# Delta rule attention and a gated feed-forward on one core: value scalings, fillers, key turns and weight conversion put in other places

## The chip, the cores and the metric

The kernel runs on one core of one Trainium2 chip. The time is device microseconds of one execution. Before the change it is 775.02 us, the median of three runs (773.91 to 776.28).

## The reference, cut to what matters

```python
k_n = k / (norm(k) + 1e-6)                      # batch 4, heads 8, sequence 768, head size 48
for t in range(768):
    y[t] = q[t] @ state
    v_old = k_n[t] @ state
    state += beta[t] * outer(k_n[t], v[t] - v_old)
x = y, heads side by side                       # 3072 x 384
h = x @ w_in                                    # 384 x 2048
out = (h * sigmoid(1.702 * h)) @ w_out          # 2048 x 384
```

The weights `w_in` and `w_out` reach the kernel as 64-bit floats and are turned into 32-bit ones on the chip by integer arithmetic; everything else is 32-bit.

## The kernel before, in words

**Units.** The sequence is cut into 6 chunks of 128 positions. A unit is one chunk of one batch with all its 8 heads: 24 units, number n = 4 c + b. For a unit the recurrence becomes a triangular solve: with the Gram matrix of its keys, `G`, and the inverses of the 32 x 32 blocks on its diagonal, `XB`, the values are solved block by block (4 blocks). A chunk's diagonal blocks are inverted for all its batches at once by `invert` (line 440), a long series of multiply and reduce pairs on VectorE (DVE). For the first chunk, which has no state, the norms of the keys are not applied to the keys but folded in as factors `zs` (lines 336 to 352); its values are multiplied by the norms with `act.mul`, one ScalarE (ACT) instruction for each head of each of the four units (lines 976 to 978).

**Hops.** `hops(a, b)` (line 985) takes two units through their four blocks in turn, 8 hops for a pair. A hop is a call of `together` (line 826): on TensorE (PE) `solve` for a block of one unit (result `psU`) and `below` for a block of the other (the product of `G` with what is solved, `psR`); then ACT copies `psU` to `US` (or `U` for the fourth unit), and DVE subtracts `psR` from `V`. The next hop needs both. The first chunk has two pairs: units 0 and 1 (loop at line 1022), then 2 and 3 (loop at line 1050). After a pair, `put_out` (line 993) makes the outputs (`psY`), the new state `ST`, and the rows `xT` for the feed-forward.

**Work written by hand between the hops.** Instructions are issued in the order of the program on every engine (`pinned`, line 100, whose line 102 carries nearly all instructions of the profile), so the order of the calls is the order of each queue:

- `fill(n)` (line 292) issues n steps of the weight conversion (`conversion`, line 203, chained by `conversions`, line 253). A piece of the weights takes five steps: p (mask of the exponent on DVE, then a Relu on ACT), t and f (fraction, DVE), or (sign, DVE, needs the Relu), fin (product, DVE). There are 9 pieces of `w_in` and 14 of `w_out`; the p of a piece is issued ahead of the last two steps of the piece before it. When a piece is done, `fetches` (line 279) may start the DMA of a later one.
- `preparing` is `keys()` (line 998): normalising the keys of units 4 to 8 (`normalize_mixed`, line 315: Square on ACT, `ssq` on DVE, a power on GpSimd (POOL), reciprocal and product on DVE), their turn by PE (`turn`, line 396: `psT`, copied to `kT`), and their Gram matrices (`gram`, line 373: `psG`, two ACT copies to `G`), with the DMAs by way of DRAM that bring the diagonal blocks to `NT`. It goes on by ticks, `ahead_of(preparing, 1)`; the tuple in line 1012 says at which tick each of the five units begins, and a unit takes a step at every second tick.
- `warm(n)` (line 132) issues n matmuls of 256 columns whose result nobody reads (`ps_warm`): fillers for PE. `NW`, `NA`, `NY`, `NU` (line 58) are their numbers.
- `feed()` (line 1037) issues half of a step of the feed-forward's first product: `hidden` (line 730) makes `ph` from `w_in` and `xT`, 3 products, and after each second half ACT applies the gate to `gT`. A product of this kernel is two matmul instructions in the profile.

**After the pairs.** The inverse of the second chunk, `invert(1)`, has 21 steps; the loop at line 1087 issues them and 25 feeds. Then come `fill(5)`, what is left of the feeds, and `woven` (line 870) for each unit to the end: a unit's hops with the two units beside it, the keys of the unit five ahead, and between them feed-forward work from `queue`, as much as `share` says. The first entry of `queue` is `both_written` (line 771), the second product of the feed-forward for units 0 and 1: `po` from `w_out` and `gT`, 16 steps of two products, each of which first issues conversion up to three steps ahead of it. The `ph`, `po` and `ps_warm` tiles share two banks.

**Buffers that the change touches.** `zs` lies in the single buffer `ksq`, which the Square of `normalize_mixed` also uses (line 951). `late_U` (line 949) takes the first 400 columns of a spare `gT` buffer of 1024 columns.

Of the kernel before, what the change touches and what calls it, by code (L numbers as in the profile page):

```python
# [8 lines left out]
F32 = mybir.dt.float32  # L9
# [9 lines left out]
def kernel(  # L19
# [21 lines left out]
    B, H, S, D = q.shape  # L41
# [4 lines left out]
    NP = H // 2  # L46
# [5 lines left out]
    HB = 2  # L52
# [2 lines left out]
    GB = 8  # L55

    XR = DP - D
    NW, NA, NY, NU = 14, 3, 34, 11
    NQ = DFF // 4
    NPC = DFF // 8  # L60
    NS = C * C + C
# [6 lines left out]
    wk = ctx.enter_context(tc.tile_pool(name="wk", bufs=2))  # L68
# [63 lines left out]
    def warm(n):  # L132
        ps = ps_moe.tile([128, 256], F32, tag="moe", name="ps_warm")
        for _ in range(n):
            pe.matmul(ps, lhsT=ones[:, 0:128], rhs=ones, start=True, stop=True)
# [156 lines left out]
    def fill(n):  # L292
        for _ in range(n):
            next(converting, None)
# [20 lines left out]
    def normalize_mixed(n):  # L315
        K = KN[n % len(KN)][:, :, 0:D]
        ksq = wk.tile([128, H, D], F32, tag="ksq", name="ksq", bufs=1)
        act.activation(ksq, K, ACT.Square)
        yield
        ssq = wk.tile([128, H], F32, tag="ssq", name="ssq", bufs=4)  # L320
        vec.tensor_reduce(ssq, ksq, axis=AX.X, op=ALU.add)
        rn = wk.tile([128, H], F32, tag="rn", name="rn", bufs=4)
        pool.tensor_tensor(rn, ssq, half, op=ALU.pow)
        yield
        vec.tensor_scalar(rn, rn, 1e-6, None, op0=ALU.add)
        vec.reciprocal(rn, rn)
        vec.tensor_tensor(K, K, rn.broadcast_to([128, H, D]), op=ALU.mult)
        yield
# [71 lines left out]
    def prepare(n):  # L400

        c, b = units[n]
        turn(n)
        yield 0.6
        G = gram(n)
        if c == 1:
            Nd = dram.tile([H * C * BS], F32, tag="Nd", name="Nd", bufs=4)
            for blk in range(NB):
                u = slice(blk * BS, (blk + 1) * BS)
                sync(out=Nd.rearrange("(h p k) -> p h k", p=C, k=BS)[u], in_=G[u, :, u])  # L410
            yield 0.0
            yield 0.9
            sync(
                out=NT[b * NB * H : (b + 1) * NB * H].rearrange("d i k -> d (i k)"),
                in_=Nd.rearrange("(d r) -> d r", r=BS * BS),
            )
            yield 0.0
            return
        Nd = dram.tile([H * NS], F32, tag="Nd", name="Nd", bufs=4)
        dma = sync if c < 3 else nc.sync.dma_start  # L420
        dma(
            out=Nd.rearrange("(h r) -> h r", r=NS)[:, 0 : C * C].rearrange(
                "h (p k) -> p h k", k=C
            ),
            in_=G,
        )
        dma(
            out=NT[b * NB * H : (b + 1) * NB * H],
            in_=Nd.rearrange("(d r) -> d r", r=NS // NB)[:, 0 : BS * C].rearrange(
                "d (i k) -> d i k", k=C  # L430
            )[:, :, 0:BS],
        )
        yield 0.9


    def spare(name):
        t = wk.tile([128, FQ, NTH], F32, tag="gT", name=name, bufs=GB)
        return t.rearrange("p f t -> p (f t)")
# [315 lines left out]
    def written(c, b0, gT):  # L754

        for i in range(HB):
            b = b0 + i
            po = ps_moe.tile([128, DM], F32, tag="moe", name="po")
            for f in range(FC):
                pe.matmul(  # L760
                    po, lhsT=gT[f // FQ][:, f % FQ, i * C : (i + 1) * C], rhs=w_out[:, f, :],
                    start=(f == 0), stop=(f == FC - 1),
                )
                if f % 2 == 1 and f < FC - 1:
                    yield 1.3
            o = wk.tile([128, DM], F32, tag="o", name="o")
            act.copy(o, po)
            nc.sync.dma_start(out=out[b * S + c * C : b * S + (c + 1) * C, :], in_=o)
            yield 1.3

    def both_written(c, gT):

        po = [ps_moe.tile([128, DM], F32, tag="moe", name="po") for _ in range(HB)]
        for n, f in enumerate(order):
            ahead = order[min(n + 3, FC - 1)]
            while ("out", ahead - ahead % 2 if 4 <= ahead < 8 else ahead) not in done:
                fill(1)
            for i in range(HB):
                pe.matmul(
                    po[i], lhsT=gT[f // FQ][:, f % FQ, i * C : (i + 1) * C], rhs=w_out[:, f, :],  # L780
                    start=(n == 0), stop=(n == FC - 1),
                )
            if n < FC - 1:
                yield 1.3
        for i in range(HB):
            o = wk.tile([128, DM], F32, tag="o", name="o")
            act.copy(o, po[i])
            sync(out=out[i * S + c * C : i * S + (c + 1) * C, :], in_=o)
        yield 1.3
# [11 lines left out]
    def run(work):  # L801
        for _ in work:
            pass

    def ahead_of(work, n):
        for _ in range(n):
            next(work, None)
# [9 lines left out]
    def new_step(n):  # L817
        if n >= len(units):
            return NoStep()
        h = n // HB  # L820
        if h not in xTs:
            xTs[h] = wk.tile([128, KC, NTH], F32, tag="xT", name="xT", bufs=3)
        steps[n] = Step(n, xTs[h])
        return steps[n]

    def together(solves, belows):

        solves = [(X, blk) for X, blk in solves if X]
        belows = [(X, blk) for X, blk in belows if X]
        psU = bank("psU") if solves else None  # L830
        psR = bank("psR") if belows else None
        for h in range(H):
            for X, blk in solves:
                X.solve(blk, h, psU)
            for X, blk in belows:
                X.below(blk, h, psR)
        for X, blk in solves:
            X.solved(blk, psU)
        for X, blk in belows:
            X.rest(blk, psR)  # L840
# [105 lines left out]
        load(n, ((KN, k),), sync)  # L946
    for blk in range(NB):
        sync(out=bI[blk::NB, 1:], in_=betas[:, 1:, blk, :])
    late_U = spare("U")[:, 0 : H * D + XR]
    pool.memset(late_U[:, H * D :], 0.0)  # L950
    zs = wk.tile([128, 6, B, H], F32, tag="ksq", name="zs", bufs=1)
    psD = [ps_seq.tile([128, B, NP, BS], F32, tag="seq", name="psD") for _ in range(2)]
    warm(NW)
    for b in range(B):
# [16 lines left out]
    pair = [new_step(n) for n in range(B)]  # L971
# [1 line left out]
        for _ in pair[n].scored:  # L973
            pass
    run(inverting)
    for s in pair:
        for h in range(H):
            act.mul(s.V[:, h, :], s.V[:, h, :], zs[:, 4, s.b, h : h + 1])
    pool.tensor_copy(landed, YB[:, 0, BS - 1 : BS])
    for s in pair[:HB]:  # L980
        s.select()
# [16 lines left out]
    def keys():  # L998

        def unit(n):  # L1000
            yield from normalize_mixed(n)
            yield from prepare(n)

        begun[2 * B] = prepare(2 * B)

        def first(n):
            yield from normalize_mixed(n)
            next(begun[n])

        work = [unit(n) for n in range(B, 2 * B)] + [first(2 * B)]  # L1010
        for t in range(24):
            for u, begin in reversed(list(enumerate((0, 3, 6, 10, 13)))):
                s = t - begin
                if s >= 0 and s % 2 == 0:
                    next(work[u], None)
            yield
        for w in work:
            run(w)

    preparing = keys()  # L1020
    path = hops(*pair[:2])
    for i in range(2 * NB):
        together(*next(path))
        fill(2)
        if i in (3, 5):
            pair[HB + (i - 3) // 2].select()
        if i > 0:
            ahead_of(preparing, 1)
        warm(NU if i < 6 else NA)
    for n, s in enumerate(pair[:2]):  # L1030
        put_out(s, 2 - n)
        load(len(KN) + n, ((KN, k),), other_queue)
# [4 lines left out]
    def feed(n=1):  # L1037
        for _ in range(n):
            while ffn and next(ffn[0], None) is None:
                ffn.pop(0)  # L1040
# [9 lines left out]
    for i in range(2 * NB):  # L1050
        together(*next(path))
        fill(2 if i < 5 else 3)
        if i > 2:
            feed()
        else:
            warm(NU)
        ahead_of(preparing, 2)
        if 3 <= i < 6:
            fetch_out(i - 3)
        if i == 5:  # L1060
            load(B, ((QP, q),), sync)
            load_values(B, sync)
# [21 lines left out]
    run(preparing)  # L1084
    run(first.scored)
    inverting = invert(1)
    for i in range(25):
        ahead_of(inverting, 1)
        feed()
    run(inverting)  # L1090
    fill(5)
    while ffn:
        feed()
    queue = [both_written(0, gTs[0]), written(*units[HB], gTs[1])]
    for n in range(B - 1, len(units) + 1):
        woven(n, 20.8 if n > 6 else 10.4)
# [32 lines left out]
```

## Time and profile before

The profiled execution:

| | |
|---|---|
| its own time | 775.35 us |
| its span, first to last instruction | 773.7 us |
| mean granted clock of TensorE | 0.973 |
| first chunk's inverse ends, first pair of hops begins | about 43 us |
| second pair begins | 70.6 us |
| second chunk's inverse, on DVE | 105.4 to 132.4 us |
| last step of the weight conversion | ends at 175.8 us |

How to read it: the page gives each engine's busy share, the granted clock in 40 slices of the span, and the chain of work that ended last. A line of a timeline is: start, duration, engine, line, operation, output<-inputs, shapes, count, and in brackets the idle time before it and what ended it. A line with count above 1 is a run of like instructions and its duration the time from the first to the last. In a windows view each line is a stretch: its length, then for PE, PEld (weight loads), DVE, ACT and POOL the busy time (and count), then the granted clock, the share of the DMA engines and their GB/s. A matmul's own duration (272 ns for a filler) is longer than the distance of two in a row (0.119 us at full clock, 0.213 at half), since they overlap.

### The profile page before, as it was taken

To read this page: it belongs to the slowest core of one execution; us is meant where nothing else is said; L and a number is where in the kernel's file an instruction comes from. 1 tells how busy PE (TensorE), PEld (TensorE's weight loads), DVE (VectorE), ACT (ScalarE), POOL (GpSimd) and SP (SyncE) were. 2 spreads that over 40 slices of the span, in tenths; PEclk is the share of its full clock that TensorE was granted. 3 is DMA by queue.
4 is the path that set the end of the run, shared out by engine and by line. 5 is a ranking of instruction groups with operands and counts; after the bars stand their busy time and mean duration, and the time that the engine had idled before them with its cause. 6 is when DMAs were issued, how large, how long until landed. Compare 5 with 4: busy or idle time off the path is not lost.

```text
span 773.7 us, 19538 instructions
## 1 busy us (share of the span) xinstructions
PE 749.6 (97%) x8537; PEld 563.1 (73%) x8537; DVE 439.9 (57%) x896; ACT 240.8 (31%) x535; POOL 129.1 (17%) x134
## 2 busy tenths in 40 slices
PE   7898999789999999999999999999999999999998
PEld 6677788456678678678678678678678677687684
DVE  6979789796965575665665665665665621000000
ACT  3464632343334223223223233223123123121110
POOL 6124210110230320220221221231210000000000
PEclk8588999999999999999999999999999999999999
DMA  9946551454342142042042042042030020000000
GB/s 163 182 63 170 132 104 27 113 145 97 76 109 56 29 101 56 24 107 56 22 101 62 22 99 65 22 99 66 22 77 12 22 45 1 17 12 1 26 1 20
DMA packets 130661, 50.78 MB, mean 66 GB/s; under 512 B 105408, under 2 KB 126016, under 8 KB 130576
## 3 DMA queue, kind: packets, MB, share of 16 engines
q1 hardware_dynamic: 128112, 41.08, 24.7%
q0 software_dynamic: 2464, 8.46, 4.4%
q8 instruction: 67, 1.10, 0.6%
q14 instruction: 18, 0.15, 0.1%
HBM read 32.08 MB, written 16.25 MB: 62 GB/s over the span
## 4 chain that ended last, share of the span: by engine, by line
PE 87%; DVE 7%; ACT 3%; issue 1%; DMA 1%; POOL 0%; SPq 0%; DVEq 0%; POOLq 0%; ACTq 0%
PE ph L102 31%; PE po L102 30%; PE psY L102 6%; PE psU L102 5%; PE psQ L102 4%; PE psG L102 4%; PE psT L102 3%; PE psR L102 3%; DVE w_out L102 2%; DVE tmp L102 2%; PE ps_warm L102 1%; ACT V L102 1%; DVE P L102 1%; DVE V L102 1%; DVE YB L102 0%
## 5 line engine op out<-in xcount | busy, mean ns | idle before, releaser
L102 PE MATMUL po<-w_out,gT 128*128 128x384 f32 x768 | 266.4, 495 | 5.5 <-DVE w_out L102 5.4
L102 PE MATMUL ph<-xT,w_in 128*128 128x256 f32 x1152 | 261.1, 383 | 0.3
L102 PEld LDWEIGHTS ph<-xT,w_in 128*128 128x128 f32 x1152 | 214.9, 190 | 32.7 <-issue 1.7
L102 PEld LDWEIGHTS po<-w_out,gT 128*128 128x128 f32 x768 | 141.4, 191 | 97.0 <-DVE w_out L102 8.3
L102 DVE TENSOR_TENSOR V<-V,psR 128x384 f32<-128x384 f32 (+2 forms) x72 | 40.1, 557 | 195.4 <-PE psR L102 190.3
L102 ACT ACTIVATE gT<-ph 128x512 f32<-128x512 f32 x96 | 56.5, 596 | 144.8 <-PE ph L102 144.7
L102 DVE TENSOR_TENSOR P<-NT,YB 64x8 f32<-64x8 f32 (+26 forms) x178 | 85.8, 482 | 4.9
L102 ACT COPY US<-psU 32x384 f32<-32x384 f32 x92 | 43.1, 469 | 133.5 <-PE psR L102 80.4
L102 PEld LDWEIGHTS psU<-V,XB 32*32 32x32 f32 x1536 | 58.7, 105 | 35.6 <-issue 27.6
L102 DVE TENSOR_REDUCE YB<-P 64x4 f32<-64x8 f32 (+27 forms) x178 | 77.2, 434 | 6.1
L102 PE MATMUL psU<-V,XB 32*32 32x48 f32 x1536 | 70.1, 203 | 2.5 <-DVE V L102 2.1
L624 POOL TENSOR_SCALAR_AFFINE_SELECT M<-M 128x1024 f32<-128x1024 f32 x20 | 25.5, 1277 | 228.2 <-DVE M L102 167.9
L102 PE MATMUL psR<-US,G 32*32 32x48 f32 x2576 | 62.7, 204 | 0.8 <-ACT US L102 0.8
L102 PEld LDWEIGHTS psR<-US,G 32*32 32x32 f32 x2576 | 53.3, 104 | 2.3 <-ACT US L102 1.2
L102 PE MATMUL psQ<-QS,kT 48*128 48x176 f32 (+1 forms) x384 | 37.6, 341 | 3.7 <-ACT QS L102 3.7
L102 DVE TENSOR_TENSOR P<-NT 64x256 f32<-64x256 f32 (+7 forms) x44 | 36.3, 825 | 0.5
L102 DVE TENSOR_REDUCE NT<-P 64x64 f32<-64x1024 f32 (+7 forms) x44 | 35.3, 803 | 1.5
L102 PEld LDWEIGHTS psQ<-QS,kT 48*128 48x128 f32 x384 | 31.1, 209 | 6.8 <-ACT QS L102 5.5
L102 PE MATMUL psG<-kT 48*128 48x128 f32 x384 | 33.0, 311 | 2.7 <-ACT kT L102 1.4
L102 PEld LDWEIGHTS psG<-kT 48*128 48x128 f32 x384 | 28.0, 210 | 6.2 <-ACT G L102 2.1
L102 ACT COPY o<-po 128x384 f32<-128x384 f32 x24 | 11.5, 478 | 61.7 <-issue 39.2
L87 POOL DMA_DIRECT2D KN<-in_k_dram x13 | 12.4, 953 | 105.9 <-PE psY L102 96.9
(100 smaller groups left out, 614.6 us busy)
## 6 DMA issues: line engine op xcount, KB each, us to landing
Nd<-G SPq DMA_DIRECT2D x16, 512.0 KB, 3.5
QP<-in_q_dram SPq DMA_DIRECT2D x24, 192.0 KB, 3.7
V<-in_v_dram SPq DMA_DIRECT2D x24, 192.0 KB, 3.1
out_dram<-o SPq DMA_DIRECT2D x24, 192.0 KB, 2.0
KN<-in_k_dram POOLq DMA_DIRECT2D x15, 192.0 KB, 3.7
NT<-Nd SPq DMA_DIRECT2D x20, 128.0 KB, 2.7
Yd<-YS SPq DMA_DIRECT2D x20, 128.0 KB, 2.5
XB<-Yd SPq DMA_DIRECT2D x20, 128.0 KB, 3.3
```

What stands on the lines that cost most here:

```text
L87: dma(out=dst[n % len(dst)][:, :, 0:D], in_=src[b, :, c * C : (c + 1) * C, :].rearrange("h p d -> p h d"),)
L102: return lambda *a, **kw: tc.keep_in_program_order(op(*a, **kw))
L624: (pool if self.n < B else nc.gpsimd).affine_select(out=self.M, in_=self.M, compare_op=ALU.is_gt, fill=0.0, base=0, pattern=[[0, H], [1, 1 ...
```

## The change

- The scalings of the values of units 2 and 3 are taken out of the block ahead of the hops and issued in hops 2 to 5 of the first pair, four heads in each hop, behind the hop's conversion steps. `zs` is moved out of `ksq` into free columns of the buffer of `late_U`.
- Fillers: 26 instead of 34 ahead of the hops, and 11 instead of 3 in the last two hops of the first pair.
- Conversion: 5 steps instead of 2 behind hop 0.
- Keys: units 5 and 6 begin a tick later, and in a tick the older unit is served first. In the second pair's hops one of the two ticks goes ahead of the feed or filler instead of both behind it.
- Behind the second inverse: 19 feeds instead of 25 are issued with its steps, and the others after it with 3 conversion steps behind each, in place of the single `fill(5)`.

```diff
--- before.py
+++ after.py
@@ -55,7 +55,7 @@
     GB = 8
 
     XR = DP - D
-    NW, NA, NY, NU = 14, 3, 34, 11
+    NW, NY, NU = 14, 26, 11
     NQ = DFF // 4
     NPC = DFF // 8
     NS = C * C + C
@@ -946,9 +946,10 @@
         load(n, ((KN, k),), sync)
     for blk in range(NB):
         sync(out=bI[blk::NB, 1:], in_=betas[:, 1:, blk, :])
-    late_U = spare("U")[:, 0 : H * D + XR]
+    room = spare("U")
+    late_U = room[:, 0 : H * D + XR]
     pool.memset(late_U[:, H * D :], 0.0)
-    zs = wk.tile([128, 6, B, H], F32, tag="ksq", name="zs", bufs=1)
+    zs = room[:, 512 : 512 + 6 * B * H].rearrange("p (s b h) -> p s b h", s=6, b=B)
     psD = [ps_seq.tile([128, B, NP, BS], F32, tag="seq", name="psD") for _ in range(2)]
     warm(NW)
     for b in range(B):
@@ -973,9 +974,12 @@
         for _ in pair[n].scored:
             pass
     run(inverting)
-    for s in pair:
-        for h in range(H):
+    def values_scaled(s, hs):
+        for h in hs:
             act.mul(s.V[:, h, :], s.V[:, h, :], zs[:, 4, s.b, h : h + 1])
+
+    for s in pair[:HB]:
+        values_scaled(s, range(H))
     pool.tensor_copy(landed, YB[:, 0, BS - 1 : BS])
     for s in pair[:HB]:
         s.select()
@@ -1009,7 +1013,7 @@
 
         work = [unit(n) for n in range(B, 2 * B)] + [first(2 * B)]
         for t in range(24):
-            for u, begin in reversed(list(enumerate((0, 3, 6, 10, 13)))):
+            for u, begin in enumerate((0, 4, 7, 10, 13)):
                 s = t - begin
                 if s >= 0 and s % 2 == 0:
                     next(work[u], None)
@@ -1021,12 +1025,14 @@
     path = hops(*pair[:2])
     for i in range(2 * NB):
         together(*next(path))
-        fill(2)
+        fill(2 if i else 5)
+        if 2 <= i < 6:
+            values_scaled(pair[HB + (i - 2) // 2], range((i - 2) % 2 * NP, (i - 2) % 2 * NP + NP))
         if i in (3, 5):
             pair[HB + (i - 3) // 2].select()
         if i > 0:
             ahead_of(preparing, 1)
-        warm(NU if i < 6 else NA)
+        warm(NU)
     for n, s in enumerate(pair[:2]):
         put_out(s, 2 - n)
         load(len(KN) + n, ((KN, k),), other_queue)
@@ -1050,11 +1056,12 @@
     for i in range(2 * NB):
         together(*next(path))
         fill(2 if i < 5 else 3)
+        ahead_of(preparing, 1)
         if i > 2:
             feed()
         else:
             warm(NU)
-        ahead_of(preparing, 2)
+        ahead_of(preparing, 1)
         if 3 <= i < 6:
             fetch_out(i - 3)
         if i == 5:
@@ -1084,13 +1091,13 @@
     run(preparing)
     run(first.scored)
     inverting = invert(1)
-    for i in range(25):
+    for i in range(19):
         ahead_of(inverting, 1)
         feed()
     run(inverting)
-    fill(5)
     while ffn:
         feed()
+        fill(3)
     queue = [both_written(0, gTs[0]), written(*units[HB], gTs[1])]
     for n in range(B - 1, len(units) + 1):
         woven(n, 20.8 if n > 6 else 10.4)
```

## The prediction

> **What bounds the kernel now.** I read the page first: shares of busy time, slices, and the chain that ended last.
>
> ```profile
> PE 749.6 (97%) x8537; PEld 563.1 (73%) x8537; DVE 439.9 (57%) x896; ACT 240.8 (31%) x535; POOL 129.1 (17%) x134
> PEclk8588999999999999999999999999999999999999
> PE 87%; DVE 7%; ACT 3%; issue 1%; DMA 1%; POOL 0%; SPq 0%; DVEq 0%; POOLq 0%; ACTq 0%
> ```
>
> TensorE (PE) carries the chain, so time can only be won where PE idles, runs at half clock or runs filler (the `ps_warm` matmuls count as busy). The chain in order of time shows that after about 176 us nearly every piece is PE; the change touches nothing there, so what is won by then should reach the end. The windows view, cut where the granted clock changes (columns: PE, PEld, DVE, ACT, POOL busy, then the clock), finds one such place:
>
> ```profile
> 56.40:59.81 3.41, 2.99 (x51) 2.10 (x48) 3.29 (x6) 1.82 (x3) 3.04 (x2) 1.00 0.04 7
> 59.81:63.23 3.42, 1.60 (x40) 1.25 (x41) 3.29 (x7) 0.47 (x1) 0.00 (x0) 1.00 1.00 223
> 63.23:66.64 3.41, 3.41 (x29) 2.76 (x27) 3.38 (x5) 2.07 (x4) 1.64 (x1) 0.51 1.02 209
> 66.64:70.05 3.41, 3.41 (x44) 3.41 (x42) 3.01 (x6) 1.26 (x4) 1.60 (x2) 0.50 0.13 26
> ```
>
> PE is busy 1.60 of 3.42 us, then works 6.8 us at half clock. VectorE (DVE) is full meanwhile. The timelines of ScalarE (ACT) and DVE show two queues that begin late:
>
> ```profile
> 39.38 7.32 ACT L102 ACTIVATE V<-V,zs 128x48 f32<-128x48 f32 x32
> 46.60 0.45 ACT L102 COPY US<-psU 32x384 f32<-32x384 f32 x1
> ...
> 48.70 0.55 DVE L102 TENSOR_TENSOR V<-V,psR 128x384 f32<-128x384 f32 x1 [4.53 <-ACT w_in L102]
> ...
> 139.18 0.55 DVE L102 TENSOR_REDUCE ssq<-ksq 128x8 f32<-128x384 f32 x1 [4.53 <-ACT ksq L102]
> ```
>
> The first copy of the first hop waits behind 32 scalings although its product ended at 45.4, and DVE stands 4.53 us before 48.70. A second DVE stop, 4.53 us before 139.18, comes just ahead of a stretch where PE waits for converted `w_out` (waits view, 132 to 176 us):
>
> ```profile
> PEld po L102 <- DVE w_out L102: 8.3, 6, 3.0
> ...
> PE po L102 <- DVE w_out L102: 5.4, 4, 2.4
> ```
>
> Windows over 138.2 to 176 us add 6.9 us of idle PE and one window at clock 0.51 (1.7 us lost), with DVE nearly full: there the conversion chain on DVE sets the pace.
>
> **What the skill says.** "TensorE: Matmul & The Clock Gate", Part 1: the array runs at half rate after a low window of some 3.4 us, and the windows run free of the program. The trace agrees: changes at 42.8, 63.2 and 70.05, multiples of 3.41 apart; 1.60 busy of 3.42 dropped the clock, 2.03 of 3.5 (148.5 to 152) did not. Same page, "Architectural detail": ACT and DVE queues are strictly first in, first out; the copy at 46.60 agrees. "ScalarE: Activation LUTs", What ACT_TABLE_LOAD costs: 280 ns + 0.833 ns per element with a pointer operand, 93 ns overlapped, which would be 227 ns for 48 elements; the trace has 7.32/32 = 229 ns, which I use.
>
> **The change, part by part.**
>
> *1. Start of the hops.* 16 of 32 scalings leave the queue: 16 x 0.229 = 3.66 us, so ACT is free at 43.04. Eight fillers fewer: the clock rises at 42.8, so those eight are fast ones, 8 x 0.119 = 0.95 us; filler ends at 43.63 instead of 44.58. `XB` of unit 0 is ready at 41.5. Solve 43.65 to 44.5, copy at 44.55 instead of 46.60, the 11 fillers of hop 0 (1.31) until 45.8, hop 1 at 45.8 instead of 46.6/47.1, its `V` subtraction at 47.4 instead of 48.70: **-1.3 us**. `fill(5)` adds three DVE steps there (0.95, 0.68, 0.95 by the rows of this stretch). The last waits for a Relu behind the copy: 45.0 + 0.94, so it ends at 46.9, before 47.4: hidden in the 4.53 us stop. Without that stop it would cost 2.6 us.
>
> *2. Hops 1 to 6.* From 48.70 to the end of the sixth subtraction, 62.87, DVE idles only 0.3 us. In the new order it does the same kinds of work there (six subtractions 3.3, ten conversion steps 8.8, normalising 1.35: 13.5). The 16 scalings now fall on ACT in hops 2 to 5, four (0.92 us) each; what is queued behind them is the next hop's `US` copy, for which `below` on PE waits. In hops 3, 4 and 5 the copy has room; in hop 2 the scalings stand behind a Relu that waits for DVE until about 51.9, so hop 3's copy comes at 53.8 and DVE waits some 0.5 us. I carry -1.2 us to the end of the sixth subtraction (61.6). Moving `zs` out of the `ksq` buffer costs nothing: it takes away the wait that the late scalings would put on `ksq`.
>
> *3. Clock.* With 11 fillers at hop 6 instead of 3 (+8 x 0.119 = 0.95, inside the 1.8 us for which PE waits there anyway) PE idles about 0.6 us, not 1.8, so I expect no drop. Then solve, key turn and two outputs run at full clock: 0.79 for 1.20, 0.44 for 1.04, 2.96 for 4.90 (the full-clock values are the same groups at 93 to 101 us): -2.95. Eleven fillers at hop 7 cost 1.31 instead of 0.64: +0.67. Next is late: a bank for the first solve of the second pair, freed by ACT copies behind one more Relu and a DVE addition behind two conversion steps: I allow +0.5. **-1.8 us**, so -3.0 when the second pair begins.
>
> *4. Order of keys.* Unit 5 and 6 are begun one tick later, within a tick the older unit goes first, and a `feed` stands between a unit's Gram product and the next turn. PE idles 0.68 us once, at 80.4, for `ACT G`, whose two copies take 1.08 us; a `feed` (1.49) covers that. All Gram and `NT` DMAs on SP keep their order, or move by a hop; the last `NT` load stays in hop 7, with about 5 us to the second inverse. A turn that now comes close behind its `KN` product may give some back: between -0.7 and +0.5, taken **-0.5**.
>
> *5. Weaving behind the second inverse.* Before it, three conversion steps more are done (0.47 + 0.27 + 0.57 = 1.3 us, in the gap at 102.7 to 104.5 where DVE waits for `psQ`). Behind it, 21 steps instead of 5 are issued, so DVE goes on where it stood: fin, t, f and so on by the spacing at 132.4 and 139.7 reach 143.5 at the end of the (4,5) piece, which now ends at 149.84, 6.4 us earlier. But the `ssq` reduction then comes last, and nothing covers the POOL power (2.03 us at 139.82) before `rn`: DVE waits about 2.2 us, -4.5 + 2.2 - 1.3 = **-3.65 us** for all that follows on DVE. PE: two `gT` activations now stand behind Relus that wait for DVE; the last comes at 139.6 instead of 137.64, and `po` of the second unit needs its bank: PE idles 1.9 us. That is hidden, since PE has 29.2 us of work at full clock for 138.2 to 176 and from 140.2 could end it by 169, while DVE ends at 172. Each `fetch_out` follows its piece earlier, and on SP still behind the `Yd`/`XB` DMAs, which end as now. From both sides: all 8.6 us of lost PE time won, at most; -1 if `rn` and the Relus hold more.
>
> Sum -1.2 - 1.8 - 0.5 - 3.65 = -7.15 us against the profiled run's own 775.35 us (span 773.7 and 1.65 around it): 768.2. That run lies 0.33 above the median, so **767.9 us**.
>
> **Rivals.** *The clock drops all the same* before the second pair, as the windows run free: the 2.95 of step 3 isn't won, the hop 7 filler costs 11 x 0.213 instead of 0.64 (+1.7), so about -1.2 + 1.7 - 0.5 - 3.65 = -3.65: 771.4. For it: busy shares of 47% and 58% lie on either side of the limit. Against: the gap shrinks to a third.
>
> *DVE keeps its lead poorly* in step 5: Relus wait for DVE, `gT` for Relus, and step 5 gives -1: 770.5.
>
> *Slower: half clock through the hops.* If the wait for hop 3's copy (scalings behind the Relu) falls into a low window, hops 4 to 7 and the first two of the second pair run at half clock, their fillers at 0.213: six windows x 1.7 us = +10.2, step 3's 2.95 lost: -7.15 + 2.95 + 10.2 = +6: 781. It decides from PE under about half busy in a window around 53 us; against it, windows there are now 88% busy and I count 1.3 us of idle at most.
>
> *The scalings only move*: if those of three of the four hops (3 x 0.92 = 2.75 us) land on the `US` chain: 770.7.
>
> **Numbers.** Forecast 767.9, 65% (its own range 765 to 770.5); clock drops 11%; poor weaving 9%; scalings on the chain 6%; slower 5%; all of step 5's 8.6 won, 763, 4%. Leaving out the last two and the edges: 764.5 to 772. A measurement tells about 0.3% (2.3 us) from no change, so faster means below 772.7: the forecast, the gain of 763 and most of three rivals, 86%; same 8%; slower 6%.
>
> **What would show it.** Step 1: first `US` copy at 44.5. Step 2: sixth subtraction ends near 61.6. Step 3: clock 1.00 from 43 us to the second pair, which begins about 67.6. Step 4: no `ACT G` wait on a turn. Step 5: no DVE stop ahead of 132 to 143 less 3.5, then one of 2 us before `rn`; last `w_out` step ends near 168.7 instead of 175.8. Wrong if half clock shows between 50 and 75 us, if `US` copies wait behind scalings, or if PE after 176 us idles more than now.

## The result, and the profile after

The changed kernel takes 772.85 us (median of 12 runs, 771.6 to 777.36) against 775.07 us for the kernel before in the same comparison (12 runs): ratio 0.9975, 95% interval 0.9953 to 0.9997. That is about 2 us faster, with an interval that ends just short of no change, and about 5 us slower than the 767.9 us predicted; it lies above the range. The profiled execution took 773.04 us (span 771.3) against 775.35 (773.7).

The page of the changed kernel, lines as shown of before: busy time, the clock, and the chain that ended last.

```profile
PE 751.0 (97%) x8545; PEld 563.6 (73%) x8545; DVE 440.6 (57%) x896; ACT 241.3 (31%) x535; POOL 128.4 (17%) x134
PEclk8588999999999999999999999999999999999999
PE 81%; DVE 10%; SPq 4%; ACT 2%; DMA 1%; issue 1%; POOL 0%; DVEq 0%; ACTq 0%
```

Nothing here tells what happened: the mean granted clock is 0.973 as before, and the slices are too coarse. The windows view, cut again within 0.15 us of where the clock changes, tells it (columns: PE, PEld, DVE, ACT, POOL busy, clock, DMA share, GB/s):

```profile
51.29:54.70 3.41, 1.96 (x58) 1.49 (x56) 3.04 (x5) 3.34 (x11) 0.49 (x1) 1.00 0.20 62
54.70:58.11 3.41, 3.41 (x43) 2.48 (x42) 3.23 (x4) 1.58 (x6) 2.24 (x2) 0.52 0.82 205
58.11:61.53 3.42, 3.42 (x43) 2.48 (x40) 2.71 (x6) 2.44 (x7) 0.00 (x0) 0.50 1.05 181
61.53:64.94 3.41, 3.41 (x26) 2.36 (x23) 3.12 (x4) 0.47 (x1) 0.00 (x0) 0.50 0.13 22
...
170.76:174.17 3.41, 3.41 (x19) 2.58 (x20) 2.14 (x4) 1.38 (x3) 0.00 (x0) 0.52 0.00 0
```

The half clock behind the first pair, which the change was to take away, is gone from there; instead it runs from about 54.8 to 65.1 us, three windows (10.2 us) in place of two (6.8 us), through hops 3 to 7. (A window is the step of 3.41 us in which the clock changes.) The one that before has at 141.8, early in the weaving stretch, stands at about 170.8 now. In the window ahead of the first drop PE is busy for 1.96 of 3.41 us. The timelines of ACT and PE show why:

```profile
51.12 0.94 ACT L102 ACTIVATE w_in<-w_in,low 128x768 int32<-128x768 int32 x1 [2.12 <-DVE w_in L102]
51.96 1.00 ACT L102 ACTIVATE V<-V,U 128x48 f32<-128x48 f32 x4
52.98 0.47 ACT L102 COPY US<-psU 32x384 f32<-32x384 f32 x1
```

```profile
51.78 0.27 PE L102 MATMUL psU<-V,XB 32*32 32x48 f32 x2
53.51 0.23 PE L102 MATMUL psR<-US,G 32*32 32x48 f32 x2 [1.45 <-ACT US L102]
...
54.31 2.07 PE L102 MATMUL ps_warm<-ident 128*128 128x256 bf16 x11
```

In hop 2 a Relu, held 2.12 us for DVE, and four scalings (`zs` appears under the name `U`, whose spare buffer it shares) stand ahead of the copy that hop 3 needs. PE stands 1.45 us, all within one window; the eleven fillers behind it then straddle the drop.

Where the time went between the profiled runs is read in four stretches. The first ends where the second pair's first solve begins, in before and then in the change:

```profile
70.64 0.86 PE L102 MATMUL psU<-V,XB 32*32 32x48 f32 x16
```

```profile
69.91 0.86 PE L102 MATMUL psU<-V,XB 32*32 32x48 f32 x16
```

So 0.7 us are won up to here, where 3.0 were predicted. From there to the start of the second inverse (105.39 and 105.54 us) it takes 35.62 instead of 34.76 us: 0.9 lost, where 0.5 were to be won. From there to the start of the last conversion step it takes 66.31 instead of 69.87 us (-3.56, predicted -3.65). Behind that 1.1 us are given back, where nothing was predicted. The sum is about -2.3, the difference of the spans.

### The profile page after: what moved, and what is told of

It is laid out like the page before. It is cut to its first block, busy times and chain, and to the rows that moved or that the text cites. A ratio compares the mean times of both kernels' runs of the same rounds, so it can differ in the third digit from the quotient of the medians.

```text
span 771.3 us, 19547 instructions
## 1 busy us (share of the span) xinstructions
PE 751.0 (97%) x8545; PEld 563.6 (73%) x8545; DVE 440.6 (57%) x896; ACT 241.3 (31%) x535; POOL 128.4 (17%) x134
## 4 chain that ended last, share of the span: by engine, by line
PE 81%; DVE 10%; SPq 4%; ACT 2%; DMA 1%; issue 1%; POOL 0%; DVEq 0%; ACTq 0%
PE po L102 30%; PE ph L102 27%; PE psY L102 6%; PE psU L102 5%; SPq L102 4%; PE psQ L102 3%; PE psG L102 3%; PE psR L102 3%; DVE w_out L102 2%; DVE P L102 2%; PE psT L102 2%; PE ps_warm L102 2%; DVE tmp L102 2%; DVE YB L102 1%; DVE NT L102 1%
## 5 line engine op out<-in xcount | busy, mean ns | idle before, releaser
L102 ACT COPY M<-psQ 128x256 f32<-128x256 f32 x68 | 22.8, 377 | 23.4 <-DVE V L102 17.3
```

Of the source, the lines that this page charges most:

```text
L102: return lambda *a, **kw: tc.keep_in_program_order(op(*a, **kw))
```

## Experiments

Theory A, as the expectations call it: the copy of hop 3, late by the Relu and the scalings, makes a low window (one in which PE is busy for too little of the 3.41 us), and the half clock eats what the hops had won. Rival B there: the clock falls wherever the scalings stand. Rival C: the late copy or the longer queue costs by itself, without the clock. Three more suspects came up on the way: the key loads, which now stand behind four `w_out` fetches on the POOL queue; the new order of the keys; the power before `rn` (the factor that norms the keys) left without cover. Each kernel is the changed one with an edit, unless it says "before +". Each batch was timed together with runs of before on the same chip:

| kernel | ratio to before, 95% | median us (runs) | median clock |
|---|---|---|---|
| the change | 0.9975, 0.9953 to 0.9997 | 772.85 (12) | 0.973 |
| scal1346 | 0.9969, 0.9956 to 0.9981 | 772.10 (22) | 0.976 |
| fill22 | 0.9984, 0.9968 to 1.0 | 773.31 (22) | 0.974 |
| weave_only | 0.9929, 0.9903 to 0.9956 | 769.60 (7) | 0.978 |
| no_weave | 0.9992, 0.9974 to 1.0011 | 773.32 (14) | 0.979 |
| kn_sp | 0.9949, 0.9932 to 0.9966 | 770.58 (15) | 0.977 |
| old_keys | 0.9916, 0.9903 to 0.9928 | 768.76 (6) | 0.980 |
| tail18 | 0.9965, 0.994 to 0.999 | 771.67 (8) | 0.975 |
| hop0_2 | 0.9914, 0.9901 to 0.9927 | 768.59 (5) | 0.980 |
| hops_only | 0.9963, 0.9952 to 0.9974 | 772.37 (19) | 0.977 |
| h2_oldkeys | 0.9901, 0.9885 to 0.9917 | 766.89 (4) | 0.980 |
| three_mended | 0.9932, 0.9915 to 0.9948 | 769.65 (6) | 0.976 |
| h2_ok_s1346 | 0.9921, 0.9905 to 0.9937 | 769.25 (5) | 0.980 |
| tm_s1346 | 0.9884, 0.9849 to 0.992 | 768.58 (6) | 0.978 |
| tm_fill22 | 0.9883, 0.9843 to 0.9923 | 767.73 (6) | 0.980 |

Before itself has a median of 774.5 to 775.8 us at a clock of 0.971 to 0.974 in these batches.

### First batch: the late copy, and the halves of the change

**scal1346**: no scalings in hop 2.

```diff
-        if 2 <= i < 6:
-            values_scaled(pair[HB + (i - 2) // 2], range((i - 2) % 2 * NP, (i - 2) % 2 * NP + NP))
+        if i in (1, 3, 4, 6):
+            g = (1, 3, 4, 6).index(i)
+            values_scaled(pair[HB + g // 2], range(g % 2 * NP, g % 2 * NP + NP))
```

> The changed kernel, with the scalings of units 2 and 3 in hops 1, 3, 4 and 6 of the first pair, where no Relu of the conversion is issued, instead of hops 2 to 5. Theory A (the 1.65 us stop of TensorE at 51.7 us, for hop 3's US copy behind a Relu and four scalings, makes the low window that halves the clock): the copy comes about 0.9 us earlier, at 52.1, the stop falls to about 0.75 us, the clock stays at 1.00 from 41 us to the second pair, which begins near 68 us instead of 70.8; time about 770, 0.35% below the changed kernel. Rival B (the clock falls because the windows run free of the program, wherever the scalings stand): half clock shows again between 50 and 70 us, the second pair begins near 70.8 and the time stays at 772.9. Rival C (the scalings cost by length of queue alone): also 772.9, with the clock at 1.00.

Half of it came true. In its profile the clock stays up through the whole first pair, the outputs of that pair end at 65.7 us instead of 70.0, and the copy of hop 3 comes at 51.75. But the time is 772.10 us where 770 was expected: the second pair, being early, meets something else. ACT's timeline there:

```profile
75.61 0.52 ACT L102 ACTIVATE ksq<-KN 128x384 f32<-128x384 f32 x1 [2.40 <-DMA KN<-in_k_dram]
76.16 0.47 ACT L102 COPY US<-psU 32x384 f32<-32x384 f32 x1
```

The Square waits 2.40 us for its keys, the copy of a hop waits behind it, PE waits 1.06 us for the copy, and the clock is down from 77.15 to 87.4 us. The drop was moved, not removed; the inverse begins at 106.68 us.

**fill22**: 22 fillers instead of 11 in hop 2, to be busy while the copy is late.

```diff
-        warm(NU)
+        warm(2 * NU if i == 2 else NU)
```

> The changed kernel with 22 fillers instead of 11 in hop 2, nothing else: hop 3's US copy stays as late as it is (53.0 us), but TensorE is busy 1.3 us of the 1.65 that it waits for it. Theory A (the low window halves the clock, and that is what the hops lose): window 51.3 to 54.7 rises from 1.96 to about 3.2 us busy, no half clock, second pair near 68.5 us, time 770 to 771. Rival C (the late copy itself is the loss): time as the changed kernel or up to 0.3 us more, 772.9.

The same outcome: no drop in the first pair, PE waits 1.32 us for `US` at 78.4, half clock from 80.3 to 87.2 us. No gain.

**weave_only**: before + the last part of the change (19 feeds, then 3 steps behind each).

```diff
-    for i in range(25):
+    for i in range(19):
...
-    fill(5)
     while ffn:
         feed()
+        fill(3)
```

> The kernel before with only the last part of the change: 19 feeds with the second inverse, the others with three conversion steps behind each, no fill(5). Theory (this part does what the changed kernel gains): the 4.53 us stop of VectorE goes, 2.2 us for the power on GpSimd come, so the last step of conversion ends about 2.3 us earlier, near 173.5; time 772.7 to 773.5, or ratio 0.997 to 0.998. Rival (its gain is given back behind 170 us by a wait or by the clock): 774.5 to 775.

This alone is 0.7%, 5.5 us, faster than before: more than expected, and ahead of the whole change, with intervals that just touch. Three conversion steps are left to cover the power before `rn` (no wait there, where 2.2 us were expected), and the stretch from the second inverse to the last conversion step takes 65.66 us, 4.21 less than in before. But not all of the 5.5 us is the weaving's. In the profiled run 2.30 us are won when the second inverse begins (103.09 against 105.39 us), ahead of everything that the edit touches: this execution had one window at half clock before the second pair where before's profile has two. Behind the conversion 1.11 us are given back, so the edit itself is worth about 3.1 us there. The median clock of its executions, 0.978 against before's 0.974 in this batch, points the same way; how much of the rest is luck isn't settled.

**no_weave**: the change without that part (the old 25 feeds and `fill(5)`).

```diff
-    for i in range(19):
+    for i in range(25):
...
+    fill(5)
     while ffn:
         feed()
-        fill(3)
```

> The changed kernel with the end of the second inverse as before: 25 feeds, then fill(5), no weaving. Theory (all other parts are worth next to nothing, since the half clock in the hops takes back what they save): second pair at about 70.8 us, DVE's second inverse at 105.5, conversion ends 1.3 us earlier than in the kernel before because three steps are done earlier, time 773.7 to 774.8. Rival (the hops' part gains its 3 us in most executions, and the profiled one was unlucky): 772 or less.

What is left of the change is worth nothing that can be measured, although its clock (0.979) is better than before's. The reason is not the expected one: its profile has no drop in the hops, and the second pair begins at 66.97 us. But it has the same wait as scal1346: the Square waits 2.33 us for the keys, PE 1.00 us at 77.9, and from the second pair to the inverse it takes 37.35 us instead of before's 34.76. So two things had to be found: the drop, and what spoils the second pair.

### Second batch: one suspect at a time

**kn_sp**: the loads of keys 7 and 8 on SP's queue instead of POOL's.

```diff
-        load(len(KN) + n, ((KN, k),), other_queue)
+        load(len(KN) + n, ((KN, k),), sync)
```

> The changed kernel with the two loads of keys behind the first pair (units 7 and 8) issued on SP's queue instead of POOL's. Theory (with three conversion steps done earlier, the four w_out fetches come ahead of these loads on POOL's queue, and the loads land 7.0 to 8.2 us after issue instead of 3.5 to 4.1; the Square of unit 7 then holds ACT, and the US copy behind it holds TensorE, 1.0 to 1.3 us where the second pair begins early): the loads land within 5 us, no Square waits for them, TensorE waits less than 0.3 us for a US copy in the second pair; time 0.5 to 1.5 us below the changed kernel's 772.85. Rival (the wait is covered in most executions, the order of the keys costs more): time unchanged within 0.5 us.

POOL's timeline of the change shows the cause that this removes:

```profile
66.04 2.28 POOL L102 TENSOR_TENSOR rn<-ssq,half 128x8 f32<-128x8 f32 x1 [9.09 <-DVE ssq L102]
68.27 2.25 POOL L102 DMA_DIRECT2D w_out<-in_moe_w_out_dram  x4
70.51 1.98 POOL L102 DMA_DIRECT2D KN<-in_k_dram  x2
```

`fill(5)` finishes a piece of `w_in` earlier, so the fetches that the piece allows are issued earlier, ahead of the keys; before, the keys went first (68.85 and 71.02, the fetches at 71.91). The tile view of `KN`, first of before, then of the change, then of this kernel:

```profile
DMA to landing us min/median/max: 3.5/4.0/4.5
```

```profile
DMA to landing us min/median/max: 7.2/7.4/7.5
```

```profile
DMA to landing us min/median/max: 2.8/3.9/4.9
```

It gains 0.26% on the change by the two ratios, with intervals that overlap a little. From the second pair to the inverse it takes 35.59 us, where no_weave and tail18, whose second pair is early too and whose keys are late, take 37.35 and 37.38. In the change's own profile the late keys cost nothing (35.62): the drop has delayed the pair by more than they need. The two faults hide each other: scal1346 and fill22, without the drop, run into the late keys, take 41.0 and 39.4 us from there to the inverse, and gain next to nothing in all. Its executions still spread, from 768.66 to 776.43 us at clocks from 0.982 down to 0.968, and the late copy is still there. The same instructions of hop 2 in its profiled run, though, cost no clock; there the copy came 0.25 us sooner (52.73), and PE waits 1.01 us for it:

```profile
51.30:54.70 3.40, 2.39 (x61) 1.88 (x60) 3.04 (x5) 3.33 (x11) 0.75 (x1) 1.00 0.35 100
54.70:58.10 3.40, 2.83 (x50) 2.13 (x48) 3.30 (x4) 1.51 (x6) 1.99 (x2) 1.00 0.83 196
```

PE is busy for 2.39 us instead of 1.96, and the next window runs at 1.00. The profiles of no_weave and tail18, which run the same instructions as the change up to the second inverse, show how little decides. No_weave's PE timeline:

```profile
48.32 0.20 PE L102 MATMUL psR<-US,G 32*32 32x48 f32 x1 [0.54 <-issue]
...
53.52 0.23 PE L102 MATMUL psR<-US,G 32*32 32x48 f32 x2 [0.89 <-ACT US L102]
```

The copy is as late as in the change (52.99 us), but PE had stood 0.54 us at 48.3 (0.87 at 48.8 in tail18), for a cause that the profile doesn't name. It so comes later to hop 3, waits 0.89 us in both, and the stops fall into two windows, each busy for 73 to 82%. The clock holds. The late copy puts the hop near the limit, and a few tenths decide in each execution.

**old_keys**: begins, order and both ticks as before.

```diff
-            for u, begin in enumerate((0, 4, 7, 10, 13)):
+            for u, begin in reversed(list(enumerate((0, 3, 6, 10, 13)))):
...
-        ahead_of(preparing, 1)
         if i > 2:
             feed()
         else:
             warm(NU)
-        ahead_of(preparing, 1)
+        ahead_of(preparing, 2)
```

> The changed kernel with the keys' ticks as before: begins 0, 3, 6, 10, 13, younger unit first, and both ticks behind the feed or filler in the second pair. Theory (the new order does not save 0.68 us but costs: turns wait 0.43 and 0.89 us for the banks of a Gram product whose ACT copies stand behind a Relu): these two waits go, one of 0.68 us comes back, time 0.5 to 1 us below the changed kernel. Rival (as predicted, the new order saves): time 0.3 to 0.7 us above.

Clearly faster than the change (0.9916 against 0.9975). Its profiled run fell into the same drop in hop 2 (PE 1.95 of 3.40 us, PE waiting 1.45 us for the copy, clock 0.973) and took 772.63 us; the other five executions have 0.978 to 0.982 and take 767.75 to 769.36. The gain is larger than expected, and much of it is clock. What the keys alone give is read from the second pair to the inverse: 34.76 us, as in before, and the two waits of the turns that the change has are gone.

**tail18**: six of the last feeds with 3 steps, the others without, so that POOL's power has steps to hide it again.

```diff
-    while ffn:
+    for _ in range(6):
         feed()
         fill(3)
+    while ffn:
+        feed()
```

> The changed kernel with 18 conversion steps woven with the feeds instead of 21. Theory (21 steps use up the look-ahead of both_written, so nothing is left to stand between ssq and the rn that waits for POOL's power; with 18, three steps do): the 1.78 us stop of VectorE at 144.6 goes, the time from the start of the second inverse on DVE to the last conversion step falls from 66.3 to about 64.5 us; time about 1.5 us below the changed kernel, 771.3. Rival (DVE's stop is covered by TensorE's own work): time unchanged.

The wait before `rn` is gone, and the stretch is 64.44 us instead of 66.31, so the 1.78 us were on DVE's path; the total (0.9965) can't be told from the change's, since the clock of its executions lies anywhere from 0.965 to 0.982.

**hop0_2**: `fill(2)` at hop 0.

```diff
-        fill(2 if i else 5)
+        fill(2)
```

> The changed kernel with 2 conversion steps behind hop 0 instead of 5. If the two theories of the POOL queue and of the look-ahead are right, taking these three steps away mends both: the keys' loads come ahead of the w_out fetches again (landing within 5 us), and three steps are left to cover POOL's power (from the inverse's start to the last step about 65.7 us, as in the kernel before with the weaving alone); time 1 to 2.5 us below the changed kernel, 770.4 to 771.8. Rival (the three early steps are a gain, as predicted at 1.3 us): time 1 us above, 774.

0.9914, 6.7 us below before and more than expected. One edit mends three things. The Relus now stand in hops 0, 1, 4 and 7 instead of 0, 0, 2, 5 and 7, so none is ahead of the scalings in hop 2 (PE is busy for 3.47 of 3.50 us from 51 to 54.5); the keys go ahead of the fetches (landing 3.9 us); and three steps are left to cover the power (the stretch takes 65.61 us).

### Third batch: do the parts add up?

**hops_only**: before + scalings, `zs`, 26 fillers and 11 in all hops, nothing else.

> The kernel before with only the first part of the change: 16 of 32 scalings moved into hops 2 to 5, zs moved, 26 fillers ahead of the hops, 11 in each hop; two steps behind hop 0, keys and tail as before. Theory (this part does save its 3 us, and the loss comes with the three early conversion steps and the key order): mean granted clock of the executions 0.976 or more against 0.974 before, time 771 to 772.5, 3 us below the kernel before. Rival (the scalings behind the Relu make the low window by themselves): mean clock 0.973 or less, time 774 to 776.

0.9963: 2.9 us, with most executions at a clock of 0.976 to 0.980. (Its profiled run was the slowest of its 19, with four windows at half clock in the hops, behind another stop of PE, 1.48 us at 49.16, so it can't show where the 2.9 us arise.)

**h2_oldkeys**: the edits of hop0_2 and old_keys together, which leaves scalings, fillers and weaving.

> The changed kernel with two conversion steps behind hop 0 and the keys' ticks as before: hops and weaving alone are left of the change. Theory (hops and weaving add up: -3 and -4.9 us): time 767 or a little below, clock 0.980 or more. Rival (the key order of the change is better once the early steps are gone): 769 to 770.

0.9901, 7.7 us below before, 5.7 below the change; it beats both kernels. All four executions lie between 766.76 and 768.18 us at 0.980 or above. Hops alone 2.9 and weaving alone 5.5 make 8.4: the two parts add, within the intervals, though the 5.5 hold some luck of the clock. The profile, which has no half clock between 39.3 and 766 us, shows both: the second inverse begins 3.57 us earlier than in before, and the stretch behind it takes 65.62 us.

**three_mended**: the changed kernel with old_keys, kn_sp and tail18, so that only the early steps of hop 0, and with them the late copy, remain.

> The changed kernel with its five steps behind hop 0, but keys' loads on SP, the keys' ticks as before and 18 woven steps. Theory (these three are all that the early steps and the key order cost; what is left is the clock): time 766.5 to 768.5 in executions with clock 0.980 or more, median 767 to 769. Rival (the early steps also lower the clock in the hops by themselves): clock 0.976 or less in more than half of the executions, median 770 to 772.

0.9932. The median lies between the two expectations, and the clock is as the rival said: 0.976 in five of six executions. The late copy remains and so does its drop:

```profile
51.00:54.50 3.50, 2.05 (x58) 1.56 (x57) 3.10 (x6) 3.33 (x11) 0.32 (x1) 1.00 0.21 67
54.50:58.00 3.50, 3.50 (x45) 2.56 (x44) 3.23 (x4) 1.99 (x7) 2.42 (x2) 0.53 1.04 219
```

**h2_ok_s1346**: h2_oldkeys with the scalings in hops 1, 3, 4 and 6 (edit of scal1346).

> As the run with two steps and the old ticks, and the scalings in hops 1, 3, 4 and 6, away from the Relus of the changed order of conversion. With two steps behind hop 0 the Relus stand in hops 0, 1, 4 and 7, so two of these hops hold one. Theory (what counts is a scaling queued behind a Relu that waits for DVE): no gain over the scalings in hops 2 to 5, 767 to 768. Rival (spreading over a longer stretch helps anyway): 766 or less.

0.9921: no gain, as the theory said, but slower than the 767 to 768 us expected. The intervals of the two kernels overlap, and the profiles don't put the difference into the hops: the second inverse begins at 101.99 us against 101.82 in h2_oldkeys, the stretch behind it takes 65.62 in both, and 1.6 us come behind the conversion, where this run has a window at half clock from 167.3 us and h2_oldkeys none. Sharing a hop with a Relu is no fault by itself either: h2_oldkeys has one ahead of the scalings in hop 4, PE waits 1.05 us for the copy at 58.25, and the clock holds.

### Fourth batch: the late copy or the low window?

Both on three_mended, where nothing else is late. **tm_s1346** takes the edit of scal1346 (the copy is early), **tm_fill22** that of fill22 (the copy stays late, PE is kept busy).

> The run with three things mended (early steps kept, keys' loads on SP, old ticks, 18 woven steps), and the scalings in hops 1, 3, 4 and 6, where with the early steps no Relu stands. Theory A (what is left of the early steps' cost is the Relu and four scalings ahead of hop 3's US copy): that copy comes at 52.0 instead of 53.0, the window around 51 to 54.5 us rises above 2.5 us busy, no half clock in the first pair's hops, clock 0.980 or more in most executions, median near 767.5. Rival B (the half clock falls on any stop of the hops, the windows being free): clock 0.976 in most executions, median near 769.6 as without the move.

> The run with three things mended, and 22 fillers instead of 11 in hop 2: hop 3's US copy stays late (53.0), but TensorE is busy through the wait. Theory A in its clock form (only the low window counts, not the late copy): no half clock in the first pair's hops, median 767.5 to 768.5. Rival C (the late copy moves the loss into the hops behind it, by the same stop one hop later): half clock again, median 769 to 770.

The same stretch of tm_s1346, then of tm_fill22:

```profile
51.00:54.50 3.50, 2.95 (x67) 2.33 (x64) 3.37 (x6) 3.33 (x9) 0.34 (x1) 1.00 0.21 57
54.50:58.00 3.50, 3.10 (x78) 2.44 (x75) 3.37 (x5) 1.46 (x5) 3.09 (x2) 1.00 0.83 215
```

```profile
51.00:54.50 3.50, 3.25 (x109) 2.63 (x109) 2.69 (x5) 3.16 (x10) 0.00 (x0) 1.00 0.02 5
54.50:58.00 3.50, 3.45 (x56) 2.69 (x54) 3.37 (x6) 2.52 (x8) 2.92 (x2) 1.00 0.98 217
```

Neither drops in the first pair. In tm_fill22 the copy still begins at 53.15 us, so it is the low window that costs the clock, not the late copy as such. The second pair begins at 66.47 and 67.38 us against 68.34 in three_mended, and all three take 34.76 us from there to the second inverse. In time they stand at 768.58 and 767.73 us against 769.65: in the direction of theory A, but the intervals of the ratios overlap, so the traces, one of each, and the clock of the executions (0.978 and 0.980 against 0.976) carry the verdict, not the time. This settles the first pair. The drop near 167 us is left in both, and tm_s1346 has one more, at 136.3 us, which makes its stretch 66.00 us where three_mended takes 64.42.

## Why the prediction was wrong, step by step

**Step 1, start of the hops: right in size, partly by luck, and two costs of `fill(5)` were missed.** The first subtraction was put at 47.4 us instead of 48.70 and came at 46.85; DVE's stop of 4.53 us ahead of it is gone. But in this execution the clock rose at 41.2 us, not at 42.8, so more of the fillers were fast, and the first copy came at 42.99 instead of 44.55 (hop0_2, where the clock rises at 42.75, has it at 44.19). And of the three steps I counted only DVE's time. They also move the fetches ahead of the key loads on POOL's queue (landing 7.4 instead of 4.0 us), which I had not followed, and put a Relu into hop 2. A filler at full clock is 0.109 us from the next in the traces, not 0.119 as I used; that changes no step by more than about 0.1 us.

**Step 2: right.** Hop 3's copy was put at 53.8 and came at 52.98; the sixth subtraction was to end at 61.6. It ends at 62.3 with the hops at half clock, and at 61.2 to 62.0 in the three profiles of the same instructions in which the clock holds (kn_sp, no_weave, tail18). hops_only measures the parts of steps 1 to 3 together, without the early steps: 2.9 us against 3.0.

**Step 3, "so I expect no drop": the step that failed.** The forecast looked only at the old place of the drop, hop 6, and filled that. The wait that step 2 itself had found was entered as 0.5 us of DVE; it is 1.45 us of PE, it makes the window from about 51.4 us low, and three windows at half clock follow. The second pair begins at 69.91 us instead of 67.6. The same instructions without the drop begin it at 66.97 (no_weave) and 67.42 us (tail18): where the clock holds, steps 1 to 3 do what was forecast, and the drop costs 2.5 to 2.9 us. My slower rival had this mechanism and place, and held 5%. It counted 1.3 us of idle PE at most, which leaves 62% of a window busy, and asked for under about half; 57% was enough. It also took six windows, where three came, so the result is a lost gain, not a loss. The first rival, a drop at the old place, comes nearest in time (771.4), but nothing dropped there.

**Step 4, order of keys: wrong sign.** It was to give 0.5 us. The `ACT G` wait didn't go; PE's timeline has two waits where before had one of 0.68:

```profile
86.47 0.65 PE L102 MATMUL psT<-ident,KN 128*128 128x128 f32 x4 [0.43 <-ACT G L102]
...
92.19 0.63 PE L102 MATMUL psT<-ident,KN 128*128 128x128 f32 x4 [0.89 <-ACT US L102]
```

From the second pair to the second inverse the change needs 0.86 us more than before, and old_keys, with the feed ahead of both ticks again, exactly as much as before. By the ratios old_keys gains 0.6% on the change, but by the price below about 3 of its 4.6 us are clock (0.980 against 0.973); with `fill(2)` the same edit is worth 0.13% by the ratios of hop0_2 and h2_oldkeys, within their intervals. "DMAs on SP keep their order" held; POOL's queue was the one to ask about.

**Step 5, weaving: right.** -3.56 against -3.65, and not by luck: its three terms can be told apart. Weaving alone takes 4.21 us off the stretch (weave_only against before; put at 4.5). The three early steps take off another 1.22 (tail18 against weave_only; put at 1.3). The power left without cover adds 1.87 (the change against tail18; put at 2.2). DVE's timeline of the change has the reduction early and the wait for POOL's power behind it, and the waits view of 132 to 180 us has the 1.9 us for `gT`:

```profile
144.08 0.55 DVE L102 TENSOR_REDUCE ssq<-ksq 128x8 f32<-128x384 f32 x1
146.41 0.17 DVE L102 TENSOR_SCALAR rn<-rn 128x8 f32<-128x8 f32 x1 [1.78 <-POOL rn L102]
```

```profile
PE po L102 <- ACT gT L102: 1.9, 1, 1.9
```

I had charged the power to the weaving; weave_only has no such wait, so it is the early steps that use up its cover. Together with that wait they are a net loss of 0.65 us here.

What I had not priced is where the half clock of this stretch would come to lie. Before, it is at 141.8, in the middle of a stretch that DVE's chain sets, and I had counted it among the losses that the lead hides; now it is at 170.8, and DVE's chain ends at 172.4, so PE has no slack left behind it. The profiles bear this out: from the start of the last conversion step to the end, the nine with a window at half clock between 167 and 176 us take 599.1 to 599.5 us, the seven without one 597.5 to 598.5. The change takes 599.48, kn_sp and old_keys, with the same instructions there and no drop, 598.53 and 598.32.

**The sum.** Scalings, fillers and weaving give 7.7 us in h2_oldkeys, where I had 7.15 for the whole. The early steps and the key order, each about 1 us by the ratios when the other is absent (0.9914 and 0.9916 against 0.9901, within the intervals), together cost 5.7, well outside them. The clock is most of the excess: 0.973 against 0.980 is three windows.

**What stays open.** Why the change itself has no clock above 0.978 in 12 executions isn't settled: no_weave, the same program up to the second inverse, has 0.982 in six of 14, and old_keys, with the same stop in hop 2, fell into the drop in one of six as far as the clock tells. What makes PE stand for some tenths ahead of hop 2 in one execution and not in another is not known; one profile of each kernel is too few. The best versions rest on 4 to 6 executions. The low window near 167 us behind the weaving was not mended.

## What to carry to other kernels

When an edit fills one low window of TensorE, go through all windows of the stretch with the new waits in them; a wait of 1.5 us that "costs 0.5" cost 2.5 to 2.9 here by the half clock behind it. Of a step that is moved ahead, follow what it releases: the DMA it triggers, whose queue that is and what stands behind it, and the wait that it had been hiding. Two faults can hide each other: here the drop hid the late keys, so that mending the drop alone gained next to nothing. And compare the parts alone, stretch by stretch as well as in total: here the last part alone came out ahead of the whole, and the stretches told what was the edit's and what the clock's.

## What the runs showed of the hardware

**Time goes with the number of half-clock windows.** Over the 266 executions of all 16 kernels here, time within a kernel falls by about 1.0 us for every 0.0022 of mean clock (correlation -0.88). One window at half clock is 3.41 / 2 / 773 = 0.0022 of the mean. The drop in the first pair, three windows for 2.5 to 2.9 us, gives the same price. The mean counts all windows, also those at the start, where PE runs fillers until the first inverse is done: before's profile has nine there and three later, the change's eight and four. That is why the two means are equal (0.973) although the change has one more where it hurts.

**A busy share of a half is no sharp limit.** The Trainium skill ("TensorE: Matmul & The Clock Gate", Part 1) puts the drop behind an idle window of some 3.4 us; the forecast read it as a low one. The windows that dropped here were not idle: PE shows 30 to 69% busy in them. I cut the 16 traces at the clock's own windows from 40 to 180 us and took those at full clock. All seven in which PE shows under 50% busy were followed by half clock, 13 of 19 between 50 and 59%, and 2 of 595 above that (61% in fill22, 69% in scal1346). In between the share doesn't decide: the change has 1.96 of 3.41 us at 51.3 and drops, 1.91 of 3.41 at 136.75 and doesn't, and before has 1.96 of 3.40 at 172.4 and doesn't. What the gate counts is not what the profile shows as busy; which it is stays open.

**DVE beside POOL.** A step that takes 0.96 us took 1.76 beside POOL's select of `M` at 55.86 (1.08 us). The skill's "SBUF — State Buffer", "Who interferes with whom", says that a DVE instruction with two SBUF inputs and a POOL instruction that reads SBUF exclude each other, and that the later one waits. The trace agrees: POOL's ends at 56.94 us and DVE's, begun at 56.00, at 57.76. In before such a pair overlaps for less (1.14 us instead of 0.96, at 59.37), so the change's DVE has 0.6 us more of this in the hops, which I had not priced.
